# A fixed instruction order per pair step with a slot plan for the fills, in the backward pass of sliding-window attention, and weighted pacing of the fills in its forward pass

## The chip, the cores and the metric

The kernel runs on one core of one Trainium2 chip. The metric is the device time of one execution, in microseconds, and lower is better. A ratio is the mean time of one kernel's fast runs over that of the other kernel's fast runs of the same rounds, so it is not quite the ratio of the medians that stand beside it. Below 1 is faster.

## The reference

Four residual blocks are computed forward, and then the gradients for the input and the weights. Blocks 0 and 2 are linear attention (A), blocks 1 and 3 sliding-window attention (B), each on the layer norm of its input.

```python
# S = 2048 tokens, D = 640, H = 32 heads of 20, window W = 256, bfloat16 in and out
def _B_ref(x, wqkv, wo):                  # sliding window: the part the change is about
    q, k, v = ...                         # (x @ wqkv) split in heads
    scores = einsum("bhqd,bhkd->bhqk", q, k) * 20 ** -0.5
    mask = (i - j >= 0) & (i - j < 256)
    p = softmax(where(mask, scores, -1e9))
    return einsum("bhqk,bhkd->bhqd", p, v)... @ wo

x = x + A(layernorm(x)); x = x + B(layernorm(x))
x = x + A(layernorm(x)); x = x + B(layernorm(x))
out, vjp = jax.vjp(f, A_x, A_wqkv, A_wo, B_wqkv, B_wo)      # returns out and all five gradients
```

## The kernel before

Tokens lie in 16 tiles of 128. The program runs these stages one after the other: the first layer forward; two "forward pairs", in each of which the heads of window block B are worked on while the previous A block's output ("front") and the next A block's input ("back") are filled in; then "backward window 3", "backward linear 2", "backward window 1" and "backward linear 0", with weight gradients between them.

**Backward window.** The work of one window block is a row of 256 *pair steps* (two heads, one query tile of 128, up to three key tiles). Two query tiles make a *chunk*: 32 steps, eight chunks. A step needs two score matmuls `s`, an exponential on ACT, masks on POOL, two matmuls `dp`, the product `ds = dp * e` on DVE, a transpose of `ds`, and some twenty small matmuls that accumulate dq, dk and dv in PSUM. Between the steps, "fills" are spread: `before` (preparing the next chunk's output gradient) and `behind` (the dense part and layer-norm gradient of the chunk two back).

```python
def drive(main, fills):                       # (cut) each fill has a rate: how many of its pieces per step
    live = [[f[0], f[1], 0.0, ...] for f in fills]
    for _ in main:
        for f in live:
            f[2] += f[1]
            while f[2] >= 1.0:
                f[2] -= 1.0
                next(f[0])
    for f in live:                            # what is left over is run at the end
        for _ in f[0]: pass

# core_chunk, one pair step (cut)
quad = self.core_dp(st, *st.q1[-st.lag1])     # dp of the step three back, high priority
s = st.pS.tile([P, 2, 512], F32, name="s")
with self.tc.high_priority():
    for j in range(2): quad.append(self.mm(s[...], Q["qT"][...], K["kT"][...], True, True, (r0, 0)))
self.together(quad, st.frees)                 # dp and s as one group of row tiles
e = st.pe.tile(...); nc.scalar.activation(e[...], s[...], ACT.Exp)
nc.gpsimd.affine_select(...)                  # masks
# core_ds: the product, and its transpose
nc.vector.tensor_tensor(out=ds, in0=st.dp, in1=e, op=ALU.mult)
if p == 1:   # every second step: five or six transposes on TensorE, copied back by DVE
    ...; nc.vector.tensor_copy(v(dT), v(ps))
else:        # every other step: a transposing DMA
    self.dma(dT, ds.rearrange("p j k -> p (j k)"), transpose=True)

# backward_window: which fills run beside chunk c
fills.append((before(c + 1), 18 / 32))
if c >= 2: fills.append((behind(c - 2), 36 / 25, 7))
drive(core(c), fills)
```

Beyond the emission order, the instruction scheduler of the framework may still reorder instructions within each engine's stream by readiness and priority.

**Forward pair.** For each of 16 tiles, eight steps of: score matmuls `sT`, exponential `eT`, two masks, and the product with v of two steps back.

```python
for t in range(TT):
    if t == 0:           fills.append((take(ahead, 34), 34 / G))     # G = 8 steps per tile
    elif t + 2 < TT:     fills.append((take(ahead, 17), 17 / G))     # "ahead" is the chain of fronts
    if prev is not None: fills.append((prev, 14 / (G - 2), 2))       # back of the tile before
    drive(self.b_core(st, lb, t, o), fills)
    prev = back(t, o)
```

The softmax here doesn't subtract the row's maximum and nothing guards it: scores larger than these inputs give would overflow.

## Time and profile before

The median is 2968.7 us (2968.57 to 2969.29 in 3 runs). The profiled execution's span is 2969.4 us.

This is the view by windows of the kernel before. Its columns are the window and its length, then the busy time of PE, PEld, DVE, ACT and POOL with the number of instructions, the granted clock of TensorE, the DMA share and the rate moved (GB/s). The windows are, in order, forward pair 0, forward pair 2, backward window 3, backward window 1, and a stretch of 330 us out of the steady part of backward window 3.

```profile
125.00:585.00 460.00, 369.79 (x4793) 246.74 (x4792) 274.73 (x731) 213.46 (x226) 170.26 (x282) 0.85 0.50 143
585.00:950.00 365.00, 277.47 (x4131) 183.33 (x4130) 177.78 (x467) 176.26 (x129) 159.82 (x263) 0.80 0.60 162
950.00:1622.00 672.00, 498.53 (x7243) 333.06 (x7244) 450.18 (x742) 274.72 (x480) 214.99 (x500) 0.70 0.67 148
1757.00:2424.00 667.00, 494.03 (x7239) 331.66 (x7239) 450.07 (x743) 273.78 (x479) 213.11 (x496) 0.71 0.64 145
1150.00:1480.00 330.00, 259.21 (x4080) 177.87 (x4078) 254.38 (x415) 153.40 (x259) 122.95 (x284) 0.76 0.74 155
```

In the last line PE is busy 79% and DVE 77% of the time: nothing is full, and the stretch is bound by waits and order. PE's figure also says less than it seems to: in the trace the accumulating matmuls start 26 ns apart while one of them is booked with 176 ns, so they overlap, and the weight loads (PEld) fill only 54%.

These are lines of the view of waits of the kernel before in the same 330 us: which engine and line waited for what, total us, times, longest us.

```profile
ACT e L615 <- PE s L162: 88.5, 75, 4.3
PE dp L162 <- DVE ds L655: 22.5, 38, 1.6
PEld L162 <- DMA dsT<-ds: 17.0, 14, 2.5
PE acc L162 <- DMA dsT<-ds: 15.4, 13, 2.4
PE dense L162 <- DMA dqT<-dqkv: 6.5, 4, 1.9
```

The second line is the loop `dp -> ds -> next dp` with DVE late; the next two are one wait, seen from PE's weight loads and from its matmuls: the accumulation needs a transpose that a DMA makes. The timeline of the kernel before shows a late `ds`. Each line has the start, the duration, the engine and the instruction.

```profile
1385.59 1.00 DVE L562 CUSTOM_DVE_ANT_0 lna<-dh,hnb 128x640 f32<-128x640 f32 x1
...
1386.52 0.48 DVE L717 TENSOR_TENSOR dq<-acc,part 128x320 bf16<-128x320 f32 x1
1386.92 0.87 DVE L565 SCALAR_TENSOR_TENSOR lna<-hnb,s,gc 128x640 f32<-128x640 bf16 x1
1387.94 0.96 DVE L655 TENSOR_TENSOR ds<-dp,e 128x768 bf16<-128x768 f32 x1
```

Two layer-norm operations of the fills (`lna`) and, between them, the end of an accumulation group (`dq`) stand in a row before `ds`, so that its step takes more than 3 us. Undisturbed steps take 1.6 to 1.9 us; the mean of a full chunk is 75 us for 32 steps, 2.35 us each.

### The profile page before, as it was taken

The numbers are of one execution on the slowest core, as the hardware profiler recorded it, in microseconds if no ns is written. First come the engines' busy times: TensorE is split into PE (matmuls) and PEld (weight loads), VectorE is DVE, ScalarE is ACT, GpSimd is POOL, SyncE is SP. The second block draws the span as 40 slices with busy tenths as digits, with TensorE's granted clock in tenths as the row PEclk, the third lists the DMA queues.
The fourth block names the chain that finished last, engine by engine and source line by source line (L and its number), as shares of the span: only waits on it lengthen the run. The fifth ranks groups of instructions, "written<-read, shape, count | busy, mean of one in ns | idle before, by whom it ended". The sixth has DMA issues, their size and how long they took to land.

```text
span 2969.4 us, 68304 instructions
## 1 busy us (share of the span) xinstructions
PE 2296.9 (77%) x28216; PEld 1520.9 (51%) x28216; DVE 1649.3 (56%) x3436; ACT 1104.7 (37%) x1693; POOL 775.9 (26%) x1584
## 2 busy tenths in 40 slices
PE   5778888668885677877776856778777759968599
PEld 4455555445553455555554644555555536447454
DVE  6656666545552467777764654777777630037100
ACT  2245555325553344444441423444444300024000
POOL 2033443325553243333330003433433200000000
PEclk9988888778886557777776985677877769989799
DMA  6264554456566567777655985676776457379852
GB/s 231 95 175 140 145 158 146 133 160 164 160 167 159 163 136 147 163 150 163 136 128 152 272 218 159 141 155 166 165 162 129 102 167 228 117 207 262 270 161 73
DMA packets 737911, 484.46 MB, mean 163 GB/s; under 512 B 484160, under 2 KB 710464, under 8 KB 737600
## 3 DMA queue, kind: packets, MB, share of 16 engines
q1 hardware_dynamic: 737600, 480.10, 62.6%
q8 instruction: 222, 3.64, 0.5%
q14 instruction: 89, 0.73, 0.1%
HBM read 216.53 MB, written 146.54 MB: 122 GB/s over the span
## 4 chain that ended last, share of the span: by engine, by line
PE 29%; DMA 14%; DVE 8%; issue 8%; POOL 4%; ACT 2%; SPq 2%; POOLq 0%; ACTq 0%; DVEq 0%
PE wg L162 12%; PE dense L162 9%; DMA dsT<-ds 4%; DVE ds L655 4%; DMA dqT<-dqa 3%; DMA dqT<-dqkv 3%; PE dp L162 2%; POOL e L618 2%; PE acc L162 2%; SPq L134 2%; DMA dqkv<-dq 2%; POOL e L622 2%; PE flip L661 1%; PE flip L208 1%; ACT e L615 1%
## 5 line engine op out<-in xcount | busy, mean ns | idle before, releaser
L655 DVE TENSOR_TENSOR ds<-dp,e 128x768 bf16<-128x768 f32 (+2 forms) x512 | 462.3, 903 | 212.9 <-PE s L162 112.5
L615 ACT ACTIVATE e<-s 128x768 bf16<-128x768 f32 (+2 forms) x512 | 395.0, 771 | 496.0 <-PE s L162 362.3
L376 ACT ACTIVATE eT<-sT 128x1536 bf16<-128x1536 f32 (+2 forms) x256 | 351.0, 1371 | 343.5 <-PE sT L162 328.9
L618 POOL TENSOR_SCALAR_AFFINE_SELECT e<-e 128x256 bf16<-128x256 bf16 x512 | 214.7, 420 | 702.4 <-ACT e L615 681.6
L378 POOL TENSOR_SCALAR_AFFINE_SELECT eT<-eT 128x512 bf16<-128x512 bf16 x256 | 164.3, 642 | 417.2 <-ACT eT L376 417.0
L162 PE MATMUL acc<-qs,ds 128*128 128x20 bf16 x2880 | 259.6, 177 | 15.3 <-DVE dq L717 12.7
L162 PE MATMUL dp<-vT,dT 32*128 32x384 bf16 (+2 forms) x1024 | 208.6, 400 | 80.0 <-DVE ds L655 62.7
L162 PEld LDWEIGHTS <-dqT 128*128 128x128 bf16 x1920 | 183.4, 105 | 162.4 <-DMA dqT<-dqkv 42.2
L162 PE MATMUL acc<-ks,dsT 128*128 128x20 bf16 x2880 | 207.1, 177 | 71.2 <-DMA dsT<-ds 70.2
L162 PEld LDWEIGHTS <-hnT 128*128 128x128 bf16 x1920 | 194.3, 107 | 129.9 <-DVE hnT L213 27.1
L162 PE MATMUL wg<-rq,lh 128*128 128x480 bf16 x1280 | 259.5, 366 | 0.0
L162 PE MATMUL acc<-ds,e 128*128 128x20 bf16 x2880 | 255.0, 175 | 0.0
L939 DVE CAST wr<-wg 128x480 bf16<-128x480 f32 (+1 forms) x36 | 21.7, 602 | 369.8 <-PE wg L162 369.8
L162 PEld LDWEIGHTS <-ds 128*128 128x128 bf16 x2880 | 213.0, 101 | 20.3 <-issue 15.9
L162 PE MATMUL dense<-WTB,dqT 128*128 128x320 bf16 x960 | 185.0, 343 | 40.2 <-DMA dqT<-dqkv 39.6
L162 PEld LDWEIGHTS <-e 128*128 128x128 bf16 x2880 | 205.0, 101 | 18.4 <-issue 10.5
L162 PE MATMUL s<-kT,qT 32*128 32x384 bf16 (+2 forms) x1024 | 208.3, 404 | 1.5 <-ACT e L615 1.1
L661 PE MATMUL flip<-ident,ds 128*128 128x128 bf16 x1440 | 177.9, 265 | 38.6 <-DVE ds L655 35.4
L162 PEld LDWEIGHTS <-dsT 128*128 128x128 bf16 x2880 | 154.6, 102 | 101.4 <-DMA dsT<-ds 81.1
L162 PEld LDWEIGHTS <-lh 128*128 128x128 bf16 x1280 | 125.2, 98 | 133.7
L162 PE MATMUL dense<-WTA,dqT 128*128 128x320 bf16 x960 | 166.9, 311 | 33.3 <-DMA dqT<-dqa 33.3
L622 POOL TENSOR_SCALAR_AFFINE_SELECT e<-e 128x256 bf16<-128x256 bf16 x448 | 192.0, 429 | 0.0
(133 smaller groups left out, 4099.9 us busy)
## 6 DMA issues: line engine op xcount, KB each, us to landing
rq<-dqkv SPq DMA_DIRECT2D x16, 1920.0 KB, 9.5
s<-s SPq DMA_DIRECT2D x32, 768.0 KB, 4.3
T<-T SPq DMA_DIRECT2D x32, 768.0 KB, 3.6
dqkv<-dq SPq DMA_DIRECT2D x32, 480.0 KB, 3.8
dqkv<-dqa SPq DMA_DIRECT2D x32, 480.0 KB, 3.7
kT<-T SPq DMA_DIRECT2D x28, 512.0 KB, 3.7
vT<-T SPq DMA_DIRECT2D x28, 512.0 KB, 4.3
ks<-s SPq DMA_DIRECT2D x28, 512.0 KB, 4.4
```

The lines of the kernel that those rows point to most:

```text
L134: return self.nc.sync.dma_start(out=out, in_=in_, transpose=transpose)
L162: return self.nc.tensor.matmul(out, lhsT=lhsT, rhs=rhs, start=start, stop=stop, skip_group_check=True, **kw)
L208: self.nc.tensor.transpose(t[0:w, j, :], src[:, c0:c0 + w], self.ident)
L376: nc.scalar.activation(e[:, :, 0:nb * P], s[:, :, 0:nb * P], ACT.Exp)
L378: nc.gpsimd.affine_select(out=dg, in_=dg, compare_op=ALU.is_ge, fill=0.0, base=0, pattern=[[0, 4], [1, P]], channel_multiplier=-1)
L615: ex = nc.scalar.activation(e[:, :, 0:cw], s[:, :, 0:cw], ACT.Exp)
L618: nc.gpsimd.affine_select(out=dg, in_=dg, compare_op=ALU.is_ge, fill=0.0, base=0, pattern=[[0, 2], [-1, P]], channel_multiplier=1)
L622: nc.gpsimd.affine_select(out=fr, in_=fr, compare_op=ALU.is_ge, fill=0.0, base=-1, pattern=[[0, 2], [1, P]], channel_multiplier=-1)
L655: st.frees.append(nc.vector.tensor_tensor(out=ds[:, :, 0:cw], in0=st.dp[:, :, 0:cw], in1=e[:, :, 0:cw], op=ALU.mult))
L661: nc.tensor.transpose(ps[:, 3 * j + i, :], ds[:, j, i * P:(i + 1) * P], self.ident)
L939: nc.vector.tensor_copy(r[:, 0:w], a[:, 0:w])
```

## The change

Its intent: write the backward window's order down by hand for PE, DVE, ACT and POOL, with at most one fill piece in each step's slot, so that fills no longer come in bursts; make three of four dS transposes on TensorE, so that accumulation no longer waits for DMA; move two kinds of work from DVE to POOL and ACT; load K and Q in quarters to save memory for double buffers of `dqT`, `hnb` and `gc`. In the forward pairs the integer counts of fill pieces are replaced by pieces with weights and a rate. The core of the diff, cut:

```diff
-def drive(main, fills):
+class Pace:                                   # (cut) at each step() the account grows by rate;
+    def step(self):                           # pieces run while it is positive, and each costs its weight
+        self.acc = min(self.acc + self.rate, 2 * self.rate)
+        while self.acc > 0:
+            w = next(self.gen, StopIteration)
+            self.acc -= w
 ...  forward_pair:
-                    fills.append((take(ahead, 17), 17 / G))
-                    fills.append((prev, 14 / (G - 2), 2))
+            fa = Pace(chain(*[front(t) for t in range(1, TT)]), 7.6 / G)     # the weights of a front add up to 7.0
+            fb = Pace(behind(), 7.3 / G)
+            for _ in range(6):
+                fa.step()                                                    # head start
             for t in range(TT):
+                drive(self.b_core(st, lb, t, outs[t]), [fa, fb])
 ...  core_step: u is this step, d the one three back, f four back, a seven back
+        # PE: dp(d), s(u);  ACT: exp(u);  DVE: ds(d);  POOL: masks(u)
+        u.by_dma = p == 0 and bi == 0         # before: every second step by DMA, now every fourth
+        if f is not None and not f.by_dma:
+            ...                               # transposes of ds(f) on TensorE
+            if f.p and f.bi:
+                nc.scalar.copy(v(f.dsT), v(ps))
+            else:
+                nc.vector.tensor_copy(v(f.dsT), v(ps))
+        if piece is not None:
+            piece()                           # the fill of this slot
+        if a is not None:
+            self.core_acc(st, l, a)
 ...  plan_before: slots of the two tiles in the chunk ahead
+        for i, (a, fl) in enumerate(((3, 8), (6, 10))):
+            plan += [(a, flip), (a + 1, prod 0), (a + 2, prod 1), (a + 2, mul),   # mul: product on POOL
+                     (fl - 1, red), (fl, flip8)]                                  # dT copy on ACT
 ...  plan_behind: two chunks later; a slot above 31 is in the chunk after
+        plan = [(2, load), (8, turn), (9, load2), (27, store_g), (33, store_dn)]  # turn: DMA transpose dqT
+        for i, (a, b, o) in enumerate(((12, 24, 30), (18, 27, 41))):
+            # six dense pieces from slot a on, which need dqT
+            plan += [(a + 7, ln1), (a + 8, ln2), (a + 8, ln3), (b, flip), (b + 1, prod 0), (b + 2, prod 1),
+                     (b + 2, mul), (b + 4, red), (o, outer), (o + 1, outer)]
 ...  backward_window
+            with self.tc.manual_schedule(engines={E.PE, E.DVE, E.Activation, E.Pool}):
+                for c in range(NC):
+                    for qr in range(4):       # K and Q slabs by quarter, five DMAs each
+                        for i, u in enumerate(self.core_steps(st, l, S, c, qr, dq)):
+                            self.core_step(st, l, u, slots[n]); n += 1
```

`ln3` is the operation that the profile shows as `gn<-dh,s,lna`, `mul` of the part behind is `prod<-dn,oa`, and `flip8` is the turn of the output gradient.

## The prediction

> **What bounds the kernel now.** The windows view gives the stages: first forward layer 125 us, forward pairs 460 and 365, backward windows 672 and 667, backward linear 135 and 146, weight gradients 201 and 199. The change acts on the pairs and the windows, 2164 of 2969 us.
>
> Backward window: 256 pair steps. In the timeline the first and last exponential lie 572 us apart: 75 us for each full chunk of 32 steps, 2.35 us a step. No engine is full (400 us of the steady part: PE 79%, DVE 76%, ACT 47%, POOL 38%), and PE's busy time overstates: accumulating matmuls start 26 ns apart though one lasts 176. Undisturbed steps take 1.57 to 1.9 us, others 3 to 5. The short ones are the loop "dp and s matmul 0.34, ds on DVE 0.95, two waits" with one dp buffer; the long ones have dense fills in bursts, DVE's layer-norm operations ahead of ds, waits for the dsT transposing DMA (about 20 us each of PE and weight-load waits in 400), or a dqkv store (4 us) followed by the dqT transpose (7.5 us). The granted clock swings between 0.5 and 1.0 (mean 0.75). [...]
> After the last exponential come 80 us, in which the last two tiles-behind run nearly in series: their buffers are single.
>
> Forward pair 0: per tile one gap of 8.4 us between exponentials, seven of 2 to 3.7 (26.5 us a tile): leftover fills are drained at the tile's end. Pair 2 has no such gap (20.4 us).
>
> **What changes, costed.** One fixed order on four engines, one fill slot per step. dS transposes by DMA fall from half of the steps to a quarter; TensorE gets 1.5 more transposes a step (about 0.08 us), ACT a copy every fourth step (0.8 us). DVE loses dT copies (0.68) and prod (0.48 each, to POOL at 1.35). Slab DMAs: twice as many, same bytes. DVE falls from about 57 to 55 us a chunk, the floor. With gaps of 0.55 us between ds operations only partly filled, and a few us of stall for dqT, I estimate 65 us a chunk: -10 us on full chunks, -8 to -11 on others, about -80 a window. Two dqT buffers let the last two tiles-behind overlap: -17. Strict startup: +5. Together -90 a window, -180 in all.
> Forward: paced fills remove the 8.4 us gaps; part of that only moves. About -2.2 us a tile in pair 0 and little in pair 2: -40.
>
> **Prediction: 2755 us**, 2650 to 2865 eight times in ten; faster by over 2%: 0.91, within 2%: 0.07, slower: 0.02.
>
> **What would show it.** Steps evenly 1.7 to 2.1 us; DVE 85% of the steady window; clock there above 0.85; waits for dsT halved; backward windows near 580 us; 60 us after the last exponential; pair 0 near 425 us without the gap, pair 2 within 15 us of 365; other stages equal.
>
> **What would make it wrong.** With a fixed order every late operand stops its engine: if dqT (four slots after its issue) or dsT regularly arrive late[...], chunks stay near 72 us. Two shared PSUM buffers could serialize flips while a dense sum holds one. ACT's copies could delay exponentials. If DVE packs without gaps, chunks reach 57 us and the total 2650.

The -180 us of the backward windows and the -40 of the forward pairs, from 2969 us, come to 2749; it doesn't explain the 6 us more of its 2755. The times of single operations in it are read off the trace before: 1.35 us is that of `prod<-ds,ob` on POOL, 0.8 that of ACT's copies of 126x768 values, 0.68 that of the dT copy on DVE, and the 0.08 for 1.5 transposes is an estimate from six that take 0.50 us together where one alone takes 0.22. The +5 for the startup is an estimate for which it gives no measurement.

## More of the kernel before

`front(t+1)` ends with two transposing DMAs `T<-s`, of which the first makes the next tile's q and k and the second its v.

In forward pair 0 a tile of eight steps takes 26.6 us, and one interval in it is long. The timeline of the kernel before at the boundary of two tiles:

```profile
313.72 1.45 ACT L376 ACTIVATE eT<-sT 128x1536 bf16<-128x1536 f32 x1 [1.71 <-PE sT L162]
...
317.32 1.94 SPq L134 DMA_TRANSPOSE T<-s  x1
...
321.69 0.29 PE L162 MATMUL sT<-T,T 32*128 32x128 bf16 x8 [0.85 <-DMA T<-s]
...
322.17 1.45 ACT L376 ACTIVATE eT<-sT 128x1536 bf16<-128x1536 f32 x1 [1.02 <-PE sT L162]
```

From one exponential to the next it is 8.45 us, and the scores that end the gap waited for the transposing DMA of this tile's q and k.

## The result, and the profile after

The kernel after takes 2925.38 us in the median (2916.07 to 2928.51 in 3 runs): ratio 0.9847, 95% interval 0.9812 to 0.9882. That is within 2%, and outside the predicted range of 2650 to 2865. The profiled span is 2926.8 us.

The view by windows of the kernel after, for the same stages and the same 330 us:

```profile
125.00:617.00 492.00, 375.84 (x4790) 250.81 (x4790) 284.41 (x728) 213.65 (x225) 170.04 (x282) 0.84 0.48 134
617.00:996.00 379.00, 286.23 (x4131) 188.35 (x4131) 184.00 (x467) 176.14 (x129) 159.85 (x263) 0.78 0.56 154
996.00:1622.00 626.00, 496.83 (x7621) 371.76 (x7621) 435.40 (x702) 326.35 (x560) 241.79 (x516) 0.77 0.60 142
1754.00:2383.00 629.00, 494.52 (x7620) 369.96 (x7620) 439.84 (x712) 327.18 (x562) 239.99 (x512) 0.78 0.58 139
1150.00:1480.00 330.00, 277.89 (x4573) 211.52 (x4571) 259.40 (x401) 194.26 (x325) 144.51 (x309) 0.84 0.62 144
```

The two forward pairs became *longer* by 32 and 14 us, and the two backward windows shorter by only 46 and 38. (The bounds of these windows were read off the timelines and don't lie at the same event in both traces, by up to 5 us: counted between first exponentials, as in the table of the experiments, pair 2 and the start of window 3 grew by 20 us.) The other stages stayed as they were: the two linear stages went from 135 and 146 us to 132 and 146, the weight gradients from 201 and 199 to 199 and 199.

The view of waits of the kernel after, same 330 us:

```profile
ACT e L568 <- PE s L163: 78.0, 66, 3.0
ACT part L645 <- DVE dq L639: 27.2, 26, 3.7
PE flip L200 <- DVE gn L763: 12.7, 5, 2.5
PE dense L163 <- DMA dqT<-dqkv: 2.9, 3, 1.3
PE acc L163 <- DMA dsT<-ds: 0.3, 1, 0.3
```

The wait for dsT is gone (15.4 to 0.3 us), where half of it had been expected to stay; e6 will show that it wasn't the move to TensorE that removed it here. In its place stand waits of up to 3.7 us for DVE. The five longest, 18.6 of the 27.2 us of `part`, lie in one slot, once in each chunk. This is that slot's timeline in the kernel after, from the exponential of slot 26 of one chunk to a little past that of slot 27:

```profile
1181.63 0.81 ACT L568 ACTIVATE e<-s 128x768 bf16<-128x768 f32 x1 [1.06 <-PE s L163]
1181.77 0.84 PE L163 MATMUL dense<-WoTA,gT 128*128 128x320 bf16 x5
...
1183.96 0.88 DVE L759 SCALAR_TENSOR_TENSOR lna<-hnb,s,gc 128x640 f32<-128x640 bf16 x1
1184.13 1.87 POOL L777 TENSOR_TENSOR prod<-dn,oa 128x640 f32<-128x640 bf16 x1 [0.86 <-DVE dn L772]
1184.87 1.81 DVE L763 SCALAR_TENSOR_TENSOR gn<-dh,s,lna 128x640 bf16<-128x640 f32 x1
1186.60 0.48 DVE L639 TENSOR_TENSOR dq<-acc,part 128x320 bf16<-128x320 f32 x1
...
1187.11 0.42 ACT L645 COPY part<-acc 128x320 f32<-128x320 f32 x1 [3.73 <-DVE dq L639]
1187.43 0.82 ACT L568 ACTIVATE e<-s 128x768 bf16<-128x768 f32 x1
...
1189.59 1.52 PE L163 MATMUL dense<-WoTA,gT 128*128 128x320 bf16 x5 [0.79 <-ACT gT L203]
```

Read it downward. The slot holds the second half of a layer-norm gradient (`lna`, `gn`), the end of an accumulation group (`dq` on DVE, then `part` on ACT), and before them `ds`, a dsT copy and `dn`: 5.1 us of DVE work in one slot, and DVE has hardly a gap in it. ACT's next exponential stands behind `part` in ACT's queue, `part` waits for `dq`, and `dq` stands behind `gn`. So the next exponential comes after 5.80 us instead of the 1.8 of a clean dense step. In the trace nothing passes `part` in the 3.73 us for which ACT stood, although the scores of that exponential were done at 1183.58 us, 3.85 us before it started. Before the stall a group of five dense matmuls takes 0.84 us (second line), after it 1.52 (last line). This pair is close to a factor of 2, and the clock records of the trace show 1.00 up to 1186.24 us and 0.50 for the 6.83 us after it. At that fall PE had stood idle for 2.0 us. But in all fifteen falls to 0.50 between 1150 and 1500 us PE was never idle for more than 2.6 us at a stretch in the 3.4 us before (worked out from the clock records and PE's instructions of the trace), and in two of them for no more than 0.22, so that the stall is not shown to be the cause. What the lower clock costs in a hand-made order isn't measured either: slots 27 to 30, which follow slot 26, took 10.1 us, and 7.7 in e18, but e18 also moved pieces out of them.

Two more things are in these lines. `gn` takes 1.81 us here, and 0.91 where it runs alone; it lies on top of POOL's `prod`, which the change moved to POOL, and which takes 1.87 us here and 1.30 for the other tile of the chunk, where no `gn` runs beside it (at 1194.28 us). `lna`, `prod` and `gn` alone take 0.88, 1.30 and 0.91 us, 3.09 together, and here they fill the 2.72 us from 1183.96 to 1186.68, only 0.37 less, although they stand on two engines. By what means the two hold each other up is not shown; that `gn` is slow because `prod` is there was tested by e16.

The mean steps of each slot over the five full chunks of window 3, worked out from the starts of the exponentials in the timeline (us):

```
slot      0    2    4    6    8    9    10   11   12   13   16   19   24   25   26   27   28   29   30   31   sum of all 32
before   3.16 2.28 2.04 1.94 1.83 2.22 1.63 1.53 4.95 2.01 1.76 2.81 3.75 2.57 1.72 3.64 1.76 1.94 3.17 4.05  75.1
after    2.00 2.18 2.41 2.32 3.19 1.55 4.60 1.47 2.97 2.44 1.56 1.42 1.32 1.87 5.80 1.96 2.76 2.79 2.63 1.38  71.8
```

The sums are means over both windows. The bursts of before are gone, and two slots of the plan, 10 and 26, are as long as the worst of them.

At the tile boundary in forward pair 0, the timeline of the kernel after:

```profile
323.87 1.45 ACT L367 ACTIVATE eT<-sT 128x1536 bf16<-128x1536 f32 x1 [0.53 <-PE sT L163]
...
330.43 1.92 SPq L135 DMA_TRANSPOSE T<-s  x1
...
334.80 0.29 PE L163 MATMUL sT<-T,T 32*128 32x128 bf16 x8 [0.94 <-DMA T<-s]
...
335.28 1.45 ACT L367 ACTIVATE eT<-sT 128x1536 bf16<-128x1536 f32 x1 [1.57 <-PE sT L163]
```

The gap that the pacing was to remove is still there; this one has grown from 8.45 to 11.41 us, with the same ending. In the mean of the third to the fourteenth tile the gap at the end of a tile grew from 8.4 to 10.0 us, and a tile takes 28.0 us instead of 26.6.

### The profile page after: what moved, and what is told of

Same layout as the page of the kernel before. It is cut to its first block, busy times and chain, and to the rows that moved or that the text cites. A ratio compares the mean times of both kernels' runs of the same rounds, so it can differ in the third digit from the quotient of the medians.

```text
span 2926.8 us, 69531 instructions
## 1 busy us (share of the span) xinstructions
PE 2310.2 (79%) x28952; PEld 1604.6 (55%) x28952; DVE 1625.9 (56%) x3340; ACT 1209.0 (41%) x1853; POOL 829.3 (28%) x1616
## 3 DMA queue, kind: packets, MB, share of 16 engines
q1 hardware_dynamic: 703552, 455.97, 58.7%
## 4 chain that ended last, share of the span: by engine, by line
PE 52%; DVE 16%; DMA 15%; issue 7%; ACT 5%; POOL 3%; SPq 2%; DVEq 0%; ACTq 0%; POOLq 0%
PE dense L163 21%; PE wg L163 12%; DVE ds L571 5%; PE flip L590 5%; DMA T<-s 4%; PE acc L163 4%; DMA dqT<-dqa 4%; PE dp L163 4%; PE flip L200 3%; ACT eT L367 2%; DMA dqT<-dqkv 2%; PE sT L163 2%; SPq L135 2%; DMA dqkv<-dq 2%; DVE dsT L597 1%
## 5 line engine op out<-in xcount | busy, mean ns | idle before, releaser
L580 POOL TENSOR_SCALAR_AFFINE_SELECT e<-e 128x256 bf16<-128x256 bf16 x512 | 221.4, 433 | 552.0 <-ACT e L568 538.7
L163 PE MATMUL acc<-slabqs,ds 128*128 128x20 bf16 x2880 | 262.5, 178 | 6.7 <-ACT part L645 5.2
L163 PEld LDWEIGHTS <-ds 128*128 128x128 bf16 x2880 | 225.8, 102 | 22.6 <-issue 7.8
L590 PE MATMUL flip<-ident,ds 128*128 128x128 bf16 x2176 | 232.2, 255 | 6.5
L163 PE MATMUL dp<-slabvT,dT 32*128 32x384 bf16 (+2 forms) x1024 | 197.9, 379 | 43.6 <-DVE ds L571 39.8
L163 PE MATMUL acc<-slabks,dsT 128*128 128x20 bf16 x2880 | 222.3, 175 | 1.6 <-DMA dsT<-ds 1.4
L590 PEld LDWEIGHTS <-ds 128*128 128x128 bf16 x2176 | 156.3, 112 | 90.5 <-issue 83.8
L163 PE MATMUL dense<-WTB,dqT 128*128 128x320 bf16 x960 | 175.1, 327 | 38.6 <-DMA dqT<-dqkv 37.6
L163 PE MATMUL s<-slabkT,slabqT 32*128 32x384 bf16 (+2 forms) x1024 | 198.1, 381 | 2.5 <-ACT e L568 1.3
L163 PE MATMUL dense<-WTA,dqT 128*128 128x320 bf16 x960 | 170.9, 316 | 36.5 <-DMA dqT<-dqa 36.4
L163 PE MATMUL dense<-WB,hnT 128*128 128x320 bf16 x960 | 185.0, 345 | 7.3 <-DVE hnT L205 6.1
```

The source lines that it names most:

```text
L163: return self.nc.tensor.matmul(out, lhsT=lhsT, rhs=rhs, start=start, stop=stop, skip_group_check=True, **kw)
L580: nc.gpsimd.affine_select(out=dg, in_=dg, compare_op=ALU.is_ge, fill=0.0, base=0, pattern=[[0, 2], [-1, P]], channel_multiplier=1)
L590: nc.tensor.transpose(ps[:, 3 * j + i, :], f.ds[:, j, i * P:(i + 1) * P], self.ident)
```

## The experiments

All of them gave correct results. Each edit is against the kernel after unless it says otherwise. This table collects what the timelines gave: pair 0 from its first exponential to that of pair 2; pair 2 from there to the first exponential of window 3; and the mean of a full chunk in both windows (us).

| run | ratio to before [95%] | pair 0 | pair 2 | chunk |
|---|---|---|---|---|
| before | 1 | 466 | 348 | 75.1 |
| after | 0.9847 [0.9812, 0.9882] | 497 | 368 | 71.8 |
| e1_oldfwd | 0.9666 [0.9632, 0.9700] | 466 | 351 | 71.7 |
| e6_dma_half | 0.9859 [0.9828, 0.9889] | 498 | 366 | 70.7 |
| e4_slots | 0.9767 [0.9734, 0.9799] | 497 | 368 | 68.1 |
| e18_slots_behind | 0.9729 [0.9700, 0.9757] | 497 | 368 | 67.8 |
| e17_slots_before | 0.9858 [0.9830, 0.9886] | 494 | 369 | 73.0 |
| e16_prod_later | 0.9837 [0.9805, 0.9868] | 497 | 366 | 71.0 |
| e5_spread_oldfwd | 0.9488 [0.9459, 0.9517] | 470 | 348 | 65.9 |
| e2_fwd_noprio | 0.9981 [0.9952, 1.0010] | 520 | 393 | 71.3 |
| e3_fwd_fixed | 1.0196 [1.0170, 1.0222] | 551 | 425 | 71.5 |
| e7_fwd_back | 0.9887 [0.9854, 0.9921] | 513 | 366 | 71.3 |
| e8_fwd_front | 0.9641 [0.9613, 0.9668] | 487 | 315 | 72.0 |
| e11_front_rate | 0.9724 [0.9683, 0.9764] | 453 | 378 | 71.6 |
| e12_front_lead | 0.9856 [0.9816, 0.9895] | 504 | 361 | 72.1 |
| e14_lead10 | 0.9882 [0.9852, 0.9912] | 491 | 377 | 71.5 |
| e15_lead4 | 0.9817 [0.9789, 0.9845] | 470 | 381 | 71.5 |
| e9_combined | 0.9365 [0.9329, 0.9402] | 463 | 317 | 65.8 |
| e10_combined_dma | 0.9448 [0.9413, 0.9483] | 464 | 317 | 66.5 |
| e13_best | 0.9349 [0.9329, 0.9370] | 457 | 314 | 65.3 |

### How much belongs to which stage

**e1_oldfwd: the change with the forward loop of before.**

```diff
-            fa = Pace(chain(...), 7.6 / G); fb = Pace(behind(), 7.3 / G) ...
+            # the loop of before: take(ahead, 17) at 17 / G, back at 14 / (G - 2), two steps late
```

> The changed kernel with the forward loop of before (bursty fills, drained at the tile's end); backward as changed. Theory: the change is two opposite parts, backward about -90 us and the paced forward about +50 us, in stages that follow one another. Then this kernel takes 2875 us (+-12), ratio to before 0.968, the pairs measure 460 and 365 us again, the windows 626 and 629. Rival: the forward loss comes from something else in the new program (shared pools, code placement); then the pairs stay near 490 and 380 and the time near 2925.

Measured: 2865.48 us beside 2963.28 for before, ratio 0.9666. The forward pairs returned to 466 and 351 us, and the backward windows stayed as in the kernel after. So the backward part of the change is worth 3.34% of 2968.7, or 99 us, and the forward part costs 1.81%, or 54 us. The theory that these are two separate effects holds.

**e6_dma_half: every second dS transposed by DMA again.**

```diff
-                    u.by_dma = p == 0 and bi == 0
+                    u.by_dma = p == 0
```

> The changed kernel with dS turned by DMA on every second step again (as before the change) in the fixed order. If the move to TensorE was a gain: TensorE saves 0.44 us in a quarter of the steps, at most 3.5 us a chunk, but waits for dsT come back (40 us in 400 before the change); chunks 73 to 77 us, total 2940 to 2980. If the move was a cost (fixed order hides the DMA, TensorE is the bound of the dense steps): chunks 69 to 70, total 2890 to 2905.

Its 0.44 us is an estimate: six transposes of `ds` take 0.51 and 0.49 us in the kernel after, at 1181.42 and 1183.70 us.

Measured: 2926.37 us, ratio 0.9859, the change's own within the interval, and a chunk of 70.7 us. Neither expectation was met. In the plan as it stands, it makes no difference to the total by which route this quarter of the transposes goes. But the trace of e6 shows two things that the total hides. The view of waits of e6, same 330 us:

```profile
PE acc L163 <- DMA dsT<-ds: 0.6, 1, 0.6
```

So with half of the steps transposed by DMA again, the wait of 15.4 us does not come back, and the move to TensorE isn't what removed it from these chunks. What is left is the fixed order, and the distance of the accumulation, which stands four steps behind the product instead of three as the program before wrote it; these two weren't separated. And the equal total is a sum of opposite parts: the first chunk of the two windows takes 57.4 and 58.7 us in e6, and 49.8 and 48.7 in the kernel after (before: 61.1 and 57.1), while the ten full chunks are 1.1 us shorter each. In the first chunk of window 3 the wait for dsT is 6.8 us in e6, 1.1 in the kernel after, and was 12.4 before. Its query tiles have one or two key tiles, so its steps are short, and its transposes by DMA are issued as two DMAs each; which of the two makes the DMA late there was not tested. e10 below repeats the comparison without the plan's stalls.

### The backward windows: which slot

**e4_slots: the later pieces of both plans spread.**

```diff
-        for i, (a, fl) in enumerate(((3, 8), (6, 10))):              # red at fl - 1, flip8 at fl
+        for i, (a, rd, fl) in enumerate(((3, 8, 11), (6, 12, 16))):
-        plan = [(2, load), (8, turn), (9, load2), (27, store_g), (33, store_dn)]
-        for i, (a, b, o) in enumerate(((12, 24, 30), (18, 27, 41))):  # ln1 at a + 7, ln2 and ln3 at a + 8
+        plan = [(2, load), (8, turn), (13, load2), (30, store_g), (40, store_dn)]
+        for i, (a, l1, l2, b, rd, o) in enumerate(((12, 19, 20, 24, 31, (35, 36)),
+                                                   (18, 27, 28, 31, 39, (41, 43)))):
```

> The changed kernel with other slots in the backward plan: reduction and flip of dS (before) at slots 8/11 and 12/16 instead of 7/8 and 9/10; layer norm, flip and reduction of the second tile behind at 27, 28, 31 and 39 instead of 25, 26, 27 and 31, and what follows from that. Theory: a chunk of 32 steps takes 72 us rather than my 65 because dependent pieces stand one slot apart, so the in-order TensorE waits for VectorE at slots 8, 10 and 26 (steps of 3.2, 4.6 and 5.8 us) and then runs at half clock for some us. Spread, those steps fall below 3 us, chunks to 64-67 us, total -80 to -110 us against the changed kernel: 2815 to 2845. Rival: TensorE's work per step is the bound (it is busy 85%); then the time only moves to other steps, chunks stay at 70 to 72, total above 2905.

What it says of TensorE is in the trace of the kernel after: in slot 26 PE stood for 2.54 us before the transposes of `gn` (12.7 us for such waits in 330), and the fifteen falls of the clock named above lie five each in slots 10 or 11, in slot 26, and in slots 0 or 1.

Measured: 2895.57 us, ratio 0.9767. Slot 26 fell from 5.80 to 2.57 us, slot 10 from 4.60 to 2.37, slot 8 from 3.19 to 1.88; but slot 12 grew, 2.97 to 4.15 in window 3. A chunk takes 68.1 us. The direction was right, and the size (0.8% by the ratios, 24 us) was between a quarter and a third of the 80 to 110 us that were expected. Since both plans moved together, two more runs took them apart.

**e17_slots_before and e18_slots_behind: one half of e4 each.** The first has only the `((3, 8, 11), (6, 12, 16))` line, the second only the lines of the plan behind.

> The change with only the part before's later pieces moved (red and flip8 to slots 11/16 and 12/16 -> mending the 4.6 us step of slot 10 alone). Theory: slots 8 and 10 lose 1.3 and 2.2 us, so 71.8 -> about 69 us a chunk, 25 us a window minus what returns in half-clock afterwards: ratio about 0.978. Rival (slot 26 carries most of the earlier run's gain): under 1 us a chunk, ratio 0.983.

> The change with only the part behind's pieces moved as in the earlier slots run (mending the 5.8 us step of slot 26 alone, with the dense sums of slot 12 still waiting for dqT). Theory: slot 26 loses 3.2 us, slot 12 gains up to 1: 71.8 -> about 69.5 us a chunk, ratio about 0.980. If the two halves add, e17's gain and this one's sum to the 0.8% of the run that did both (0.9767 against 0.9847).

Measured for e17: 2926.73 us, ratio 0.9858. Nothing was gained. Slots 8 and 10 did fall, to 1.50 and 2.78 us in window 3, but slots 9, 11 and 12 grew from 1.55, 1.47 and 2.97 to 2.51, 2.28 and 4.76: the five together are 13.8 us in both. Half of what slots 8 and 10 lost came back in slots 9 and 11, between and at the new places of the moved pieces. For the other half, in slot 12, the view of waits of e17, same 330 us, says what took its place; this line stands at 2.9 us in the kernel after:

```profile
PE dense L163 <- DMA dqT<-dqkv: 12.9, 4, 4.3
```

The dense pieces of slot 12 wait for the transposed gradient. Its DMA is issued in slot 8 and reads what a store has written: on the chain of the kernel after the store runs from 1141.52 us for 4.88 us and the transpose from 1146.41 for 7.63. In the median of the kernel after the store of 960 KB is done 5.1 us after its issue and the transposed load of the same 960 KB after 7.0 (the directions differ and other transfers were under way), so a plan of slots that gives both the same time comes out 1.9 us short here, about a step. When slots 8 and 10 are quicker, slot 12 is reached earlier and waits longer. The long slots 8 and 10 had hidden this wait, and so mending what the profile shows in them was worth nothing by itself.

Measured for e18: 2888.59 us, ratio 0.9729, chunk 67.8. The half that mends slot 26 (5.80 to 2.57, and slots 27 to 30 from 10.1 together to 7.7, though this plan also moves the second tile's flip and products out of 27 to 29) carries all of the gain of e4. Whether the halves add is not resolved: their ratios would give 0.9858 + 0.9729 - 0.9847 = 0.9740, and e4's interval begins at 0.9734.

**e16_prod_later: only the POOL product of the part behind moved by one slot.**

```diff
-                     (b + 2, mul), (b + 4, red), ...
+                     (b + 3, mul), (b + 4, red), ...
```

> The change with one thing moved: the a_grad product on POOL (prod<-dn,oa) of the part behind, one slot later, so that it no longer lies in the slot in which DVE runs gn. Theory (gn takes 1.81 instead of 0.91 us because it meets a POOL operation [...]): gn 0.91 everywhere, slot 26's step 5.8 -> 4.9 us, 71.8 -> about 71 us a full chunk, some 7 us a window, 14 in all: ratio to before about 0.980. Rival (the collision hides behind other waits of that slot): gn 0.91 but the chunk stays within 0.3 us and the ratio at 0.985. Second rival: the product meets another DVE operation of slot 27, which slows instead.

The groups of instructions named `gn` in this window, with count and the shortest, median and longest time in ns, first of the kernel after and then of e16:

```profile
L763 DVE SCALAR_TENSOR_TENSOR gn<-dh,s,lna x32: 875/907/1807, 1171.9 to 2373.7; 128x640 bf16<-128x640 f32 x32
```

```profile
L763 DVE SCALAR_TENSOR_TENSOR gn<-dh,s,lna x32: 874/886/907, 1169.8 to 2361.6; 128x640 bf16<-128x640 f32 x32
```

The longest `gn` fell from 1807 to 907 ns by nothing but taking `prod` out of its slot, and slot 26's mean from 5.80 to 4.88 us. The collision is therefore shown, and both numbers of the theory were met. Slot 27 stayed at 1.96 us in the mean, so the second rival, a new collision there, is not seen. Its effect on the total was not resolved: 2920.40 us, ratio 0.9837 with an interval of 0.9805 to 0.9868 holds both the 0.980 of the theory and the 0.985 of the rival. A chunk was 0.8 us shorter in the mean, all of it in window 3; in window 1 the slots 12 and 13 took back what slot 26 gave.

**e5_spread_oldfwd: a wider spread, with the forward loop of before.** On top of e1:

```diff
+        for i, (a, rd, fl) in enumerate(((3, 11, 16), (6, 15, 20))):
+        plan = [(2, load), (8, turn), (18, load2), (33, store_g), (44, store_dn)]
+        for i, (a, l1, l2, b, p1, rd, o) in enumerate(((15, 23, 24, 28, 31, 35, 40), (21, 31, 32, 36, 39, 43, 44))):
```

Here the dense pieces begin in slot 15 instead of 12, and no slot has two heavy DVE pieces or one together with an accumulation's end.

> The changed kernel with the forward loop of before (as e1, 2865 us) and a wider slot plan than e4: the dqT transpose still at slot 8, its first dense at 15 instead of 12; reductions and flips of dS at 11/16 and 15/20; second tile behind: layer norm 31 and 32, flip 36, products 37 and 39, reduction 43, outer products 44 and 45. Theory: what e4 left of my 65 us a chunk is the dqT wait at slot 12 (the steps of 3.6 to 4.2 us[...]) and pieces that hold one of the two PSUM buffers; with three more slots chunks take 64 to 66 us and the total is 2815 to 2835, ratio 0.953. Rival: a chunk is bound by the sum over steps of the slowest engine of each step [...]; then chunks stay at 67 to 69 and the total at 2840 to 2855.

Measured: 2817.38 us beside 2970.14, ratio 0.9488; a chunk of 65.9 us, which is the predicted 65 within a microsecond. No wait for dqT is left in the view of waits, slots 8 to 12 take 10.1 us together instead of 13.8 (they also hold fewer pieces now), and the longest mean step is 3.3 us. Since e5 differs from e1 in the slots alone, the plan's slots are what separated the chunk from its predicted length. Between exponentials the two windows lost 75 us against e1; by the ratios the kernel gained 53, because the later pieces made the part after the last exponential some 12 us longer in each window.

### The forward pairs: what ends the gap

**e2_fwd_noprio: the score matmuls without high priority.** The first theory was that the scores, which have priority, reach PE's queue before their q and k are there, and hold up the fills that make them.

```diff
-            with self.tc.high_priority():
-                for i in range(nb): ... self.mm(s[...], ...)
+            for i in range(nb): ... self.mm(s[...], ...)
```

> The changed kernel without the high priority of the forward score matmuls. Theory: in both kernels the scheduler lets these matmuls overtake the paced fills, so the next tile's q and k are turned just in time whatever the pace, and each tile ends in a gap of 8 to 12 us. Without the priority the emitted pace governs: the gap falls under 5 us and tiles take about 25 us instead of 28.5, pair 0 near 440 us, total near 2880. Rival: the tile period is set by the amount of TensorE work and its clock; then the gap moves into the other seven intervals and pair 0 stays at 480 to 495 us, total 2915 to 2930.

Measured: 2959.84 us, ratio 0.9981, which is 1.3% worse than the change itself. The gap at the tile's end did fall, mostly to 2 or 3 us, but the time moved to other places in the tile: a tile of pair 0 took 29.3 us in the mean of the fifteen, and 27.1 in the kernel after. The theory fell, and the time lies above the range of the rival too.

**e3_fwd_fixed: PE's order fixed in the forward pair as well.**

```diff
+            with self.tc.manual_schedule(engines={E.PE}):
                 for t in range(TT): ...
```

> The changed kernel with TensorE's order in the forward pairs fixed as emitted (as the change does in the backward windows), pace unchanged. Theory of the overtaking scores: front now runs over a tile ahead, no interval above 6 us, pair 0 at 420 to 450 us, total near 2870. Rival (work-limited): pair 0 480 or more. Third outcome: a fixed order stalls at every late operand, pair 0 over 500 us.

Measured: 3025.17 us, ratio 1.0196. From the view of PE's waits of e3, between 260 and 560 us (in the same stretch, before had 8.9 us for the same wait, and the kernel after 19.5):

```profile
PE flip L200 <- DVE hn L221: 43.8, 18, 3.2
```

In the order as written, the transposes of `hn` come directly after the layer norm that makes it, so a fixed PE stands and waits, as the third outcome of the expectation said. This is the same trap as in the backward slots.

**e7_fwd_back and e8_fwd_front: which of the two paces.**

```diff
-            fb = Pace(behind(), 7.3 / G)                 # e7
+            fb = Pace(behind(), 6.9 / (G - 2))
```

```diff
-            fa = Pace(chain(...), 7.6 / G)               # e8
+            fa = Pace(chain(...), 7.0 / G)
-            for _ in range(6):
+            for _ in range(8):
```

> The changed kernel; only the rate of the trailing fills of the forward pairs is raised from 7.3/8 to 6.9/6 a step, so that a tile's trailing work ends within six steps, as before the change, and does not spill into the next tile. Theory: the spilled trailing work takes TensorE from the next front, whose q and k the next tile waits for; then tiles go back to 26.5 us and the total to 2870 to 2885. Rival: something else in the pacing; tiles stay at 28 to 29, total 2915 to 2930.

> The changed kernel; only the leading fills of the forward pairs are altered: rate 7.0/8 instead of 7.6/8 and 8 steps ahead instead of 6, so the front is emitted exactly two tiles ahead, as before the change, and doesn't run away. Theory: the runaway front (up to three tiles ahead by the end) gets priority over the trailing work and fills the queues with operations that are not ready; tiles go back to about 26.5 us, total 2875 to 2890. Rival: as e7's; total 2915 to 2930.

Measured: e7 2935.04 us, ratio 0.9887, with pair 0 at 513 and pair 2 at 366 us: no gain. e8 2862.03 us, ratio 0.9641, a real gain, but in the other pair than the theory said: pair 2 fell from 368 to 315 us, below the 348 of before, and pair 0 only from 497 to 487. The windows of 175 us in pair 2, first of the kernel after and then of e8:

```profile
780.00:955.00 175.00, 140.74 (x2057) 92.94 (x2055) 87.63 (x221) 89.25 (x62) 79.21 (x130) 0.78 0.55 147
```

```profile
715.00:890.00 175.00, 155.16 (x2708) 109.26 (x2709) 110.74 (x291) 116.50 (x81) 103.66 (x170) 0.94 0.71 189
```

And the exponentials of e8 there:

```profile
812.23 1.45 ACT L367 ACTIVATE eT<-sT 128x1536 bf16<-128x1536 f32 x1 [0.54 <-PE sT L163]
814.21 1.45 ACT L367 ACTIVATE eT<-sT 128x1536 bf16<-128x1536 f32 x1 [0.53 <-PE sT L163]
816.18 1.45 ACT L367 ACTIVATE eT<-sT 128x1536 bf16<-128x1536 f32 x1 [0.53 <-PE sT L163]
```

In such steps the stage runs at the pace of its loop of exponential and scores, 1.97 us a step (1.45 busy, 0.53 to wait for the next scores, of which there is one buffer); the mean over a tile is 2.19. The granted clock in the window rose from 0.78 to 0.94.

**e11_front_rate, e12_front_lead, e14_lead10, e15_lead4: rate and head start one by one.** e11 has only the rate 7.0 / G with 6 steps of head start, e12 only the 8 steps at 7.6 / G, e14 and e15 have 7.0 / G with 10 and 4 steps.

> The changed kernel with only the front's rate lowered, 7.0/8 instead of 7.6/8, still 6 steps ahead (e8 altered both). If the runaway is the cause, all of e8's gain is here: about 2862 us, pair 2 near 316. If the head start is the cause, none of it: 2915 to 2930. In between if both count.

> The changed kernel with only the head start enlarged, 8 steps instead of 6, rate as in the change. Counterpart of e11: near 2862 us if the head start is the cause, 2915 to 2935 if the runaway is (it is then a little worse).

> The changed kernel, front rate 7.0/8, 10 steps ahead (a lead of 1.47 fronts at each tile's start; 8 steps gave 1.18, 6 gave 0.82). If a larger constant lead is what helps: pair 2 stays at 315 to 320 us and pair 0 at 487 or less. If what counts is where in the tile the front's chains fall (phase), the times jump without order: pair 2 may be back at 350 to 380, pair 0 anywhere between 450 and 500.

> The changed kernel, front rate 7.0/8, 4 steps ahead (lead 0.71). If lead is what counts, pair 2 is no better than with 6 steps (378 us) and pair 0 close to 453. If phase counts, either may change by over 20 us.

Measured: 2891.26 us (0.9724), 2929.55 (0.9856), 2921.29 (0.9882) and 2902.24 (0.9817). At the rate 7.0 / G, with a head start of 4, 6, 8 and 10 steps, pair 0 takes 470, 453, 487 and 491 us, and pair 2 takes 381, 378, 315 and 377. It isn't monotone: in each pair one of the four head starts is best. The arithmetic of the paces says what the rate does. The weights of a front add up to 7.0, so at 7.6 / G the fronts run away: their lead, counted in pieces at each tile's start, drifts from 0.88 of a front to 1.94 over the pair, and at 7.0 / G it stays at one value (0.71, 0.82, 1.18 and 1.47 for the four head starts). So at 7.0 / G every tile has the same phase between the front's pieces and the eight steps. That the head start matters and that more isn't better is measured; that it is the phase that counts is a reading of this and was not shown, and *why* pair 0 does best at 0.82 and pair 2 at 1.18 stays open. In pair 0, e11 halves the gap at the tile's end, from 10.0 to 5.0 us in the mean, but the other seven intervals grow from 17.9 to 20.9 us together: more than half of what the gap loses only moves.

### Together

**e9_combined**: the slots of e5, the loop of before in pair 0, the pace of e8 in pair 2. **e10_combined_dma**: the same with `u.by_dma = p == 0`. **e13_best**: the slots of e5 in the change, with

```diff
-            fa = Pace(chain(...), 7.6 / G)
+            fa = Pace(chain(...), 7.0 / G)
-            for _ in range(6):
+            for _ in range(8 if last else 6):            # last: pair 2
```

> The wide slots of e5, the forward loop of before in pair 0 and the pacing of e8 (front exactly two tiles ahead) in pair 2. Theory: the three gains lie in different stages and add: e5 measured 2817 us, e8's pair 2 is about 50 us shorter than before's; so 2760 to 2780 us, ratio 0.932, pair 2 at 310 to 320 us. Rival: e8's gain depends on its pair 0 or on the code in front of it; then pair 2 stays near 365 and the total near 2815.

> As e9 with dS turned by DMA on every second step, as before the change. With the plan's own stalls (e6) the choice made no difference. If TensorE is now the bound of the dense steps, a chunk gets 2 to 3.5 us shorter, total -30 to -50 us against e9; if the transposing DMA arrives late [...], a chunk gets 2 to 5 us longer, total +30 to +70; no difference within 15 us if both happen.

> Wide slots of e5; front rate 7.0/8 with 6 steps ahead in pair 0 (as e11, 453 us between first exponentials) and 8 in pair 2 (as e8, 315 us). If the stages add as in e9: e9's 2786 us less 10, so 2768 to 2785, ratio 0.933.

Measured: e9 2786.36 us beside 2977.44, ratio 0.9365; e10 2808.62, ratio 0.9448; e13 2763.89 beside 2955.13, ratio 0.9349, faster than both kernels. The gains of the two stages add up, although e9 missed its range by 6 us: pair 2 is 31 us shorter than before's (348 to 317), not 50. With the stalls gone, e10 against e9 shows that the move of the transposes to TensorE is worth 22 us, which is none of the three outcomes that were expected. Nearly all of it, 21 us, lies in the first chunks of the two windows (46.3 and 47.6 us in e9, 56.0 and 58.8 in e10); a full chunk differs by 0.7 us. The waits in the first chunk of window 3 of e10 (in that of e9 this line stands at 0.8 us):

```profile
PE acc L190 <- DMA dsT<-ds: 9.6, 12, 1.8
```

The windows of 330 us, first of e9 and then of e10 (both run 40 to 47 us past the last exponential):

```profile
1150.00:1480.00 330.00, 274.67 (x4578) 212.91 (x4575) 259.32 (x407) 188.59 (x322) 144.92 (x303) 0.85 0.66 151
```

```profile
1150.00:1480.00 330.00, 270.63 (x4474) 206.14 (x4472) 245.35 (x372) 192.62 (x330) 148.26 (x309) 0.82 0.83 175
```

e10 has a DMA share of 0.83 instead of 0.66 and less busy time on PE and DVE; in 330 us that lie wholly before the last exponential (1042 to 1372 us of e9, 1049 to 1379 of e10) it is the same picture: DMA 0.84 against 0.66, DVE 254 against 274 us.

## Why the prediction was right or wrong

The sum was -180 us from the backward windows and -40 from the forward pairs. Measured were -99 and +54.

**Right.**
- The waits for dsT: "halved" was predicted, and they all but vanished (15.4 to 0.3 us in 330). For the full chunks this was luck as far as the reason goes, since in e6, with the DMA's share of transposes as before, they stand at 0.6; in the first chunk of a window the route does matter (e6, e10).
- The part from the last exponential to the issue of the last store of `dn`: 82 us before, 65 after in each window, which is the -17 predicted (60 us had been named). Startup rose by 1 us, not by 5.
- Other stages stayed equal, and stages are serial, so what they gain or lose adds: the six stage differences (+32, +14, -46, -3, -38, -2) sum to the difference of the spans.
- The warning "with a fixed order every late operand stops its engine ... chunks stay near 72 us" hit the number (71.8), though it stood among the risks and got a chance of 9% together with all the others. The number is luck in part: the late operands that it names are dqT and dsT, with 2.9 and 0.3 us of waits in 330, and the operand that came late was DVE's, in slot 26.

**Wrong step 1: "With gaps of 0.55 us between ds operations only partly filled, and a few us of stall for dqT, I estimate 65 us a chunk".** The estimate added up DVE's busy time (55 us) and put a margin on it. With one exponential per step in a fixed order, the steps' lengths add up: the slots of the kernel after come to 71.8 us a chunk, and slot 26 took 5.80 us with 5.1 us of DVE's work in it, and 4.88 in e16, where `gn` takes 0.9 us less. That each of the 32 steps is as long as its own fullest engine was not worked out; slot 26 was. An average over 32 steps can't show such a slot, but the plan's numbers can: 26 = a + 8 of the second tile, = b + 2 of the first, and also a step in which an accumulation group ends (every fourth step). All three were known before the run, and I had not laid the pieces into the slots. What the runs showed in place of the estimate: 71.8 us a chunk; mending the crowded slot 26 gives 4.0 of it back (e18: 67.8); in it the collision of `gn` with the product moved to POOL is 0.9 us (e16); the dense sums of slot 12 come too early for dqT, which absorbs about half of what is mended in slots 8 and 10 (e17); with these and other pieces moved further, the chunk is 65.9 (e5). From exponential to exponential the windows lost 36.5 and 26.4 us and not 80 each, and about half of that lies in the first two chunks, where the plan has only the pieces of `before`. DVE is busy 79% of the 330 us, not 85%. So the size was right for a good plan and wrong for this one.

**Wrong step 2: "Forward: paced fills remove the 8.4 us gaps".** The cause I had given the gap, "leftover fills are drained at the tile's end", was wrong by plain arithmetic: 17 pieces at 17/8 a step leave nothing over after eight steps. The gap's last link was in the trace before (`sT <-DMA T<-s`): this tile's q and k arrive last. The new pacing left that wait as it was and chose a rate above the weight of a front (7.6 for 7.0), so that the lead of the fronts drifted from tile to tile, and the gap grew from 8.4 to 10.0 us in the mean. Pair 0 became 492 us instead of the predicted 425 and pair 2 379 instead of 365. With the rate of 7.0 alone changed, pair 0 is 44 us shorter than in the kernel after (e11, 497 to 453) and the gap 5.0 us; so the rate is shown to count there, but e8 has the same rate and 487 us, and what the right lead does stays open. That pacing can help was right only with another rate and head start (e8, e11, e13), and pair 0 didn't come near 425 in any run.

**Where the expected gain went,** then: some 80 us in the two windows, of which the slots of e5 bring back 53 by the ratios, so that not all of it is shown to be the plan's stalls; and 94 us between what was expected of the forward pairs and what they gave.

**Open.** Why the best head start differs between the two forward pairs. What the fixed order alone is worth: no run has the new plan with the scheduler left free, or the old fills in a fixed order. The slabs in quarters and the double buffers were not tried alone. The weights of the pieces in the linear stages changed too, with no effect seen (135 to 132, 146 to 146 us).

## What to carry to other kernels

Before you fix an order by hand, lay every piece into its slot with its measured time, add them up per slot and engine, and look at the largest slot, not the average: heavy pieces, their dependants and the operations that end a group must not meet in one slot (slot 26 here: 5.80 us, and 2.57 once spread, in e4), and a DMA's consumer belongs behind its real arrival time (dqT here: 7.0 us after its issue). When you mend a stall and nothing is gained, look for the wait that took its place; here mending two slots was worth nothing, since the time came back in the slots beside them, half of it as a wait for a DMA, and mending the third was worth all of it. And before you say what causes a gap, follow the last release in the trace and do the arithmetic of the loop that you blame.
